# Projecting q and k in two passes of 1024 tokens, each by seven products of half matrices

## The chip, the cores and the metric

The kernel runs on one core of a Trainium2 chip. A core has a matrix engine (TensorE, PE in the profile; its weight loads are listed as PEld), a vector engine (VectorE, DVE), a scalar engine (ScalarE, ACT), GpSimd (POOL) and SyncE (SP), which issues most of the transfers; transfers can also be issued from the queues of ScalarE and of GpSimd. Each engine runs its instructions in the order in which they were written and waits on semaphores for the others. The metric is the device time of one execution in microseconds, lower is better.

## The reference: attention and a routed expert layer, mixed by a gate

The input x has 2048 tokens of 1024 numbers, in fp32. Three things are computed from it:

```
g = sigmoid((x * gate_w).sum(-1))                 # one number per token
q, k, v = split(x @ wqkv)                         # 32 heads of 32 columns each
a = softmax(q k^T / sqrt(32)) v, heads joined, @ wo
b = for each token and each of 32 heads: the best of 8 first keys and the best of 8
    second keys give an expert of 64;  sum of gelu(x . u[e]) * v[e]
out = g * a + (1 - g) * b
```

The part that is changed is `x @ wqkv` for q and k (1024 columns each), the sums of the gate, and a bound on the scores that the softmax uses as its shift.

## The kernel before

**Precision.** A number is kept as two parts, hi (a copy in the matrix engine's fast 32-bit format, made by ScalarE) and lo (number minus hi, by VectorE); the helper `split` (lines 92 to 94) issues both. A product of two matrices is three matmuls: hi by hi, hi by lo and lo by hi.

**The stages.** In order: q and k are projected and stored to DRAM in hi and lo parts (lines 99 to 360); the router's matmuls over 16 tiles of 128 tokens (`router_mm`, L394), beside which VectorE and GpSimd find each token's experts; the values v (from line 625, seven products of half matrices there already: class `Halves`, L617); attention, head by head (L968, L978, L989); the output projection.

**The projection.** x lies transposed (features on the partitions) in SBUF, all 2048 tokens, as hi and lo parts (`xh`, `xl`, four tiles of 512 tokens each). q and k have eight chunks of 128 columns each. Chunk 0 of both is computed while x arrives: for each of the eight 128-feature rows of x (`kc`), ScalarE and VectorE split the row (`split_x`), and TensorE runs 24 matmuls on it (`mm0`, L213), into eight PSUM banks. The other 14 chunks (loop at L322) are four blocks each of 24 matmuls (L329): 56 blocks. The weights of a chunk are loaded two chunks ahead (`load_w`) and split (`split_w`). After each block, `evac` (L135) splits the result into hi and lo, takes the largest absolute value of hi (L141) and keeps the running maximum per column (`amax`); the stores to DRAM go out on ScalarE's queue one block later.

**What lies between the blocks.** The router's keys are folded into its weights: 32 steps of `fold` (L267), four at a time after every fourth block (blocks 8, 12, ... 36), each with a 1 MB load (`load_wq`, four buffers) and four fp32 matmuls with 32 weight columns (L274). After four of them the sum is copied (`wt`, L280), transposed on TensorE one block later (`fold_t`, L288), copied again (L291) and stored. From block 40 on, VectorE adds up x times the gate's weights (`gate`, L311 and L313: 64 instructions of 512 columns); four matmuls in the router stage sum that over the partitions (`gate_sums`, L464). From block 42 the router's weights are loaded back and split (L356).

**The bound.** For each head, the sum over its 32 columns of max|q| times max|k| is an upper bound of its scores (lines 363 to 370 and `bound`, L448). If any bound is above a limit, `exact_maxima` (L475) computes the real maxima in a long extra stage; with these inputs it is jumped over.

The order of the work is written out by hand: what each engine does next is the order of the calls in the code.

## Time and profile before

| | |
|---|---|
| median of 3 runs (lowest to highest) | 1852.4 us (1852.29 to 1852.59) |
| the profiled execution | 1853.26 us, of which the profile's span is 1851.4 us |
| TensorE's first projection matmul | 6.68 us after the span's start |
| the router's first matmul (the projection is over) | 390.60 us |
| TensorE busy in the span | 99% |
| granted TensorE clock, mean | 1.000 |

The profile's page gives, for each engine, its busy time; the span in 40 slices with the busy share of each engine in tenths; and groups of instructions by line of the code, with the count, the busy time, the mean duration of one, and how long the engine stood idle just before them, with the instruction that ended most of that wait. A matmul's duration includes the pipeline; matmuls overlap, so that the distance from one start to the next is what one costs. The timeline lists single instructions by start and duration in microseconds; idle time and what ended it stand in brackets.

### The profile page before, as it was taken

The numbers are of one execution on the slowest core, as the hardware profiler recorded it, in microseconds if no ns is written. First come the engines' busy times: TensorE is split into PE (matmuls) and PEld (weight loads), VectorE is DVE, ScalarE is ACT, GpSimd is POOL, SyncE is SP. The second block draws the span as 40 slices with busy tenths as digits, with TensorE's granted clock in tenths as the row PEclk, the third lists the DMA queues.
The fourth block names the chain that finished last, engine by engine and source line by source line (L and its number), as shares of the span: only waits on it lengthen the run. The fifth ranks groups of instructions, "written<-read, shape, count | busy, mean of one in ns | idle before, by whom it ended". The sixth has DMA issues, their size and how long they took to land.

```text
span 1851.4 us, 26129 instructions
## 1 busy us (share of the span) xinstructions
PE 1841.2 (99%) x10131; PEld 1128.1 (61%) x10131; DVE 1365.8 (74%) x1219; ACT 1198.3 (65%) x1492; POOL 170.1 (9%) x214
## 2 busy tenths in 40 slices
PE   9999999999999999999999999999999999999999
PEld 7877777887888744444444444444444444447787
DVE  4522224978887788888888888888888888896674
ACT  4211111201233399999999999999999999993221
POOL 0000000025401100000000000000000000000000
PEclk9999999999999999999999999999999999999999
DMA  5777784423237687767777777877777777875851
GB/s 216 284 255 257 271 286 136 135 66 105 80 123 249 244 186 159 175 153 174 164 172 178 167 185 162 187 164 178 177 164 175 161 180 167 181 158 181 288 176 57
DMA packets 122853, 332.10 MB, mean 179 GB/s; under 512 B 15988, under 2 KB 57220, under 8 KB 98472
## 3 DMA queue, kind: packets, MB, share of 16 engines
q1 hardware_dynamic: 85048, 180.58, 31.9%
q0 software_dynamic: 17584, 112.08, 28.0%
q10 hardware_dynamic: 20096, 37.76, 6.5%
q8 instruction: 80, 1.31, 0.3%
q14 instruction: 45, 0.37, 0.1%
HBM read 158.65 MB, written 72.10 MB: 125 GB/s over the span
## 4 chain that ended last, share of the span: by engine, by line
PE 60%; DMA 3%; ACT 1%; DVE 0%; issue 0%; SPq 0%; DVEq 0%; ACTq 0%
PE ring L968 27%; PE o L989 25%; PE pa L617 6%; PE ring L1002 1%; DMA accd<-P 1%; DMA out<-rb 1%; DMA accd<-rd 1%; PE pa L1180 1%; DMA rb<-rd 1%; DMA smd<-ssb 0%; ACT P L978 0%; SPq L75 0%; PE pa L1173 0%; DVE V L1242 0%; DMA V<-od 0%
## 5 line engine op out<-in xcount | busy, mean ns | idle before, releaser
L978 ACT ACTIVATE P<-ring 128x1024 f32<-128x1024 f32 (+2 forms) x1031 | 912.4, 983 | 14.7 <-DMA accd<-P 2.6
L1018 DVE TENSOR_TENSOR acc<-acc,P 128x2048 f32<-128x2048 f32 x319 | 731.0, 2291 | 75.1 <-ACT P L978 49.6
L989 PE MATMUL o<-P,V 128*32 128x512 f32 x3840 | 464.8, 599 | 0.0
L968 PE MATMUL ring<-Q,K 98*128 98x512 f32 x1024 | 272.0, 407 | 0.1
L968 PE MATMUL ring<-z,z 98*128 98x512 f32 x1020 | 270.9, 407 | 0.7 <-ACT accd L978 0.6
L968 PEld LDWEIGHTS ring<-Q,K 98*128 98x128 f32 x1024 | 182.0, 188 | 144.2 <-ACT P L978 73.3
L968 PEld LDWEIGHTS ring<-z,z 98*128 98x128 f32 x1020 | 181.2, 188 | 143.4 <-ACT P L978 71.0
L989 PEld LDWEIGHTS o<-P,V 128*32 128x32 f32 x3840 | 98.8, 109 | 223.0 <-issue 214.1
L93 ACT ACTIVATE hi<-bk 128x512 fp32r<-128x512 f32 x64 | 37.6, 598 | 242.1 <-PE bk L329 226.7
L94 DVE TENSOR_TENSOR lo<-bk,hi 128x512 fp32r<-128x512 f32 x64 | 44.2, 690 | 182.2 <-ACT hi L93 178.1
L329 PE MATMUL bk<-xh,whi 128*128 128x512 f32 x448 | 176.2, 393 | 0.1
L329 PE MATMUL bk<-xh,wlo 128*128 128x512 f32 x448 | 174.4, 389 | 0.0
L329 PE MATMUL bk<-xl,whi 128*128 128x512 f32 x448 | 174.4, 389 | 0.0
L1011 POOL DMA_DIRECT2D accd<-P x95 | 81.5, 858 | 930.1 <-ACT P L978 356.3
L1016 DVE TENSOR_TENSOR acc<-P,P 128x2048 f32<-128x2048 f32 x32 | 73.4, 2293 | 72.8 <-ACT P L978 72.8
L329 PEld LDWEIGHTS bk<-xh,whi 128*128 128x128 f32 x448 | 84.1, 188 | 24.1 <-issue 6.7
L329 PEld LDWEIGHTS bk<-xh,wlo 128*128 128x128 f32 x448 | 84.1, 188 | 17.8
L329 PEld LDWEIGHTS bk<-xl,whi 128*128 128x128 f32 x448 | 84.2, 188 | 17.1
L1021 DVE TENSOR_TENSOR acc<-acc,accd 128x2048 f32<-128x2048 f32 x32 | 73.1, 2285 | 0.0
L978 ACT ACTIVATE accd<-ring 128x1024 f32<-128x1024 f32 (+2 forms) x64 | 62.2, 1032 | 2.5 <-PE ring L968 2.4
L617 PE MATMUL pa<-woh,acc 128*128 128x512 f32 x192 | 62.2, 389 | 0.0
L398 ACT ACTIVATE xu<-bk 128x64 f32<-128x64 f32 x16 | 3.6, 224 | 76.5 <-PE bk L394 76.5
(246 smaller groups left out, 1862.5 us busy)
## 6 DMA issues: line engine op xcount, KB each, us to landing
accd<-P POOLq DMA_DIRECT2D x95, 1024.0 KB, 7.6
wqt<-in_wq SPq DMA_DIRECT2D x32, 1024.0 KB
z<-kdh SPq DMA_DIRECT2D x32, 256.0 KB
z<-qdh SPq DMA_DIRECT2D x32, 256.0 KB
V<-vd SPq DMA_DIRECT2D x32, 256.0 KB
K<-kdh SPq DMA_DIRECT2D x32, 256.0 KB
Q<-qdh SPq DMA_DIRECT2D x32, 256.0 KB
od<-osb SPq DMA_DIRECT2D x32, 256.0 KB
```

The costliest lines, as they stand in the source:

```text
L93: nc.scalar.activation(hi, src, AF.Copy)
L94: (on or nc.vector).tensor_tensor(out=lo, in0=src, in1=hi.bitcast(F32), op=OP.subtract)
L329: nc.tensor.matmul(ps, a[:, kc, :], b[n][:, kc, :], start=first, stop=last)
L617: nc.tensor.matmul(ps, self.a[a][i][:, k, :], self.b[b][j][k], start=(not first and k == 0 and i == j == 0), stop=(k == HC - 1 and i == 1))
L968: on_ring(nc.tensor.matmul(ring[:, i, :], K[:98, kt * 128:(kt + 1) * 128], Q[:98, qc * 512:(qc + 1) * 512], start=True, stop=True), i)
L978: on_ring(nc.scalar.activation(P[h, kt][:, q0 * 512:(q0 + m) * 512].rearrange("p (a m) -> p a m", a=m), ring[:, i:i + m, :], AF.Exp, scale ...
L989: nc.tensor.matmul(O[h][32 * qc:32 * qc + 32, :], Vt[g][:, kt, 32 * j:32 * j + 32], p[:, qc * 512:(qc + 1) * 512], start=(kt == 0), stop=( ...
L1002: yield nc.tensor.matmul(ps[32 * qc:32 * qc + 32, :], ones, src[:, qc * 512:(qc + 1) * 512], start=(src is srcs[0]), stop=(src is srcs[-1]))
L1011: nc.gpsimd.dma_start(ACCD[h], P[h, kt], accum_op=OP.add)
L1016: nc.vector.tensor_add(ACC[h], P[h, 0], P[h, kt])
L1018: nc.vector.tensor_add(ACC[h], ACC[h], P[h, kt])
L1021: nc.vector.tensor_add(ACC[h], ACC[h], ACCD[h])
```

## The change

The projection is done in two passes of 1024 tokens: the second half of the tokens first, then the first half. In a pass, q chunk c and k chunk c together are a matrix of 2 x 2 weight quarters A11, A12 (q, features 0 to 511 and 512 to 1023), A21, A22 (k), and x is one of 2 x 2 quarters B11, B12 (features 0 to 511, tokens in two groups of 512), B21, B22. Their product is computed as seven products of quarters (P1 to P7, function `product`, 12 matmuls each) instead of eight, with four sums of weight quarters (S1 to S4, made for every chunk on VectorE, then split) and four differences of quarters of x (T1 to T4, made once a pass on VectorE, then split). The results are joined by seven additions on VectorE per chunk. A pass has eight steps: step 0 and step 8 (`plain_mm`) use the eight plain products, with the quarters of x as they are split; steps 1 to 7 and 9 to 15 are `unit`s with seven products. The second pass takes the chunks in reverse order, so that steps 7 and 8 share weights.

Within a unit the weights of the next unit are summed and split, one quarter after each product, in single places. `evac` splits a result; a Square on ScalarE with a running sum (`accum_out`) takes the place of the maxima on VectorE, one evacuation later together with the stores (`run_late`). The bound becomes the root of the product of the sums of squares over 512 tokens, its maximum over the four groups; the limit is as it was.

The folds go two at a time, after 13 of the steps and in the middle of units 4, 10 and 13, with two loads of 1 MB after each (four half-size buffers, that is, as much as one such fold uses). The copy `wt` is put in the place of `u4`, and the transposes stand right after P1 of the next unit.

The gate's sums become 32 fp32 matmuls per pass with one weight column and 256 tokens each, on the raw x (`gate_sums`), before the last eighth of step 0 and before step 8. The 64 instructions on VectorE and the four matmuls in the router stage go.

At the end of the first pass the second half of x is loaded and split in unit 7 (hooks of unit 7). The parts of x that the router and the values need are made again: one quarter in unit 15 (`split_n1`), four in the router stage at tiles 1, 2, 3 and 5 (`split_rx`), from five loads of 1 MB. The router's weights are split in unit 15.

The core of the diff:

```diff
+    PASS = (dict(B11="xh3", B21="xl0", B22="xl1", B12="xh0", T1="xl2", T2="xh0", T3="xh2", T4="xh1",
+                 ra="xh1", rb="xh2"),
+            dict(B11="xh0", B21="xl0", B22="xl1", B12="xh2", T1="xh1", T2="xh2", T3="xl2", T4="xh3",
+                 ra="xh3", rb="xl2"))
+    TOK0 = (S // 2, 0)
...
+    sq = const.tile([128, 2, KC, NQ], F32, name="sq")
...
-    def evac(which, c, n, ps, parts):
-        m = parts[0].shape[1] // 512
-        hi, lo = (t[:, n % m * 512:(n % m + 1) * 512] for t in parts)
-        split(hi, lo, ps)
-        mx = ev.tile([128, 1], F32, name="m", bufs=8)
-        nc.vector.tensor_reduce(mx, hi.bitcast(F32), axis=AX.X, op=OP.max, apply_absolute_value=True)
-        am = amax[:, which, c:c + 1]
-        if n == 0:
-            nc.vector.tensor_copy(am, mx)
-            nc.vector.tensor_max(am, am, mx)
-        store_parts()
-        if n % m == m - 1:
-            for dst, t in zip(QKD[which], parts):
-                stores.append((dst[128 * c:128 * c + 128, (n + 1 - m) * 512:(n + 1) * 512], t))
...
+    CHUNK = list(range(KC)) + list(range(KC))[::-1]
...
+    def x_parts(place, src=None, pool=None):
+        t = (pool or (xp8 if place == "xl3" else xp)).tile([128, 2, HC, 512], F32R, name=place)
+        if src is not None:
+            split(t[:, 0], t[:, 1], src)
+        return t[:, 0], t[:, 1]
+    def x_quarter(p, name):
+        X[name] = x_parts(PASS[p][name], XR[name], xp)
+    def x_sum(p, name):
+        a, b = dict(T1=("B12", "B11"), T3=("B22", "B12"), T2=("B22", "T1"), T4=("B21", "T2"))[name]
+        out = dict(T1="B11", T3="B12", T2="B22", T4="B21")[name]
+        XR[name] = XR[out]
+        nc.vector.tensor_tensor(out=XR[name], in0=XR[a], in1=XR[b], op=OP.subtract)
...
+    def x_raw_at(kc, c):
+        n, c = divmod(c, 512)
+        return XR[f"B{1 + kc // HC}{1 + n}"][:, kc % HC, c:c + 256]
+    def gate_sums(p):
+        pz = bank_at(6)
+        for kc in range(KC):
+            for q in range(4):
+                nc.tensor.matmul(pz[32 * q:32 * q + 1, :256], gw[:, kc, :], x_raw_at(kc, 256 * q),
+                                 start=(kc == 0), stop=(kc == KC - 1))
+        for q in range(4):
+            row = slice(32 * q, 32 * q + 1)
+            nc.scalar.activation(XR["zs"][row, :], pz[row, :256], AF.Copy)
+            c = TOK0[p] + 256 * q
+            dma(ZD[:, c:c + 256], XR["zs"][row, :], nc.gpsimd)
...
+    def w_sum(u, name):
+        r = wraw[u]
+        a, b, op, out = dict(
+            S1=("A21", "A22", OP.add, None), S2=("S1", "A11", OP.subtract, "A11"),
+            S3=("A11", "A21", OP.subtract, None), S4=("A12", "S2", OP.subtract, "A21"))[name]
+        a, b = r[a], r[b]
+        r[name] = r[out] if out else wr.tile([128, HC, 128], F32, name=name, bufs=1)
+        nc.vector.tensor_tensor(out=r[name], in0=a, in1=b, op=op)
+    def w_parts(u, name, src=None):
+        split(*w_place(name), wraw[u][src or name])
...
+    late = []
+    def run_late():
+        for f, *a in late:
+            f(*a)
+        late.clear()
+    def squares(out, src, which, c, n):
+        nc.scalar.activation(out, src, AF.Square, accum_out=sq[:, which, c, n:n + 1])
+    def evac(which, c, n, src, ps):
+        hi, lo = (ev.tile([128, 512], F32R, name=part) for part in ("hi", "lo"))
+        split(hi, lo, src)
+        run_late()
+        late.append((squares, ps, src, which, c, n))
+        for dst, t in zip(QKD[which], (hi, lo)):
+            late.append((dma, dst[128 * c:128 * c + 128, n * 512:(n + 1) * 512], t, nc.scalar))
...
+    PLAIN = {(0, 0): "A11", (0, 1): "A12", (1, 0): "S4", (1, 1): "A22"}
...
+    FACTORS = dict(P1=("A11", "B11"), P2=("A12", "B21"), P3=("S4", "B22"), P4=("A22", "T4"),
+                   P5=("S1", "T1"), P6=("S2", "T2"), P7=("S3", "T3"))
+    def product(name):
+        ps = bank_at(prod_no[0] % 6)
+        prod_no[0] += 1
+        a, b = (m[f] for m, f in zip((AW, X), FACTORS[name]))
+        for k in range(HC):
+            for i, j in ((0, 0), (0, 1), (1, 0)):
+                nc.tensor.matmul(ps, a[i][:, k, :], b[j][:, k, :],
+                                 start=(k == 0 and i == j == 0), stop=(k == HC - 1 and i == 1))
+        return ps
...
+    def fold():
+        for _ in range(2):
+            if i == 0:
+                fold_ps[:] = [bank_at(6)]
+            t = wq_t.pop((n, 0)), wq_t.pop((n, 1))
+            for quad in range(4):
+                nc.tensor.matmul(ps[32 * quad:32 * quad + 32, :], kpad[:, quad % 2, i, :],
+                                 t[quad // 2][:, quad % 2, :], start=(i == 0), stop=(i == 3))
+        if i == 3:
+            wt = ev.tile([128, 512], F32, name="u4", bufs=1)
+            nc.scalar.activation(wt, ps, AF.Copy)
+            pending.append((n // 4, wt))
+        for m in range(n + 1, min(n + 3, 32)):
...
+        if kc == 3:
+            load_w(1)
+        if kc == 4:
+            for n in range(2):
+                load_wq(n)
+        if kc == 5:
+            w_sum(1, "S1")
+            w_sum(1, "S3")
+            w_parts(1, "S1")
+            kpad_diffs()
         if kc == KC - 1:
-            split_w(0, 1)
-            load_w(1, 1)
-
-            xr.close()
-            ev0 = Pool("ev0")
-        order = [(n, i) for i in range(3) for n in range(NQ)]
+            gate_sums(0)
+            x_sum(0, "T1")
+            x_quarter(0, "T1")
+            w_parts(1, "A11")
+            w_sum(1, "S2")
+            w_parts(1, "S2")
+            w_sum(1, "S4")
+            w_parts(1, "S4")
+            for name in ("T3", "T2", "T4"):
+                x_sum(0, name)
...
+    def plain_evac(u, w, n):
+        evac(w, CHUNK[u], TOK0[u // KC] // 512 + n, b0[w, n], b0[w, n])
+    def after_plain(u, done):
+        rest = [(w, n) for n in range(2) for w in range(2) if (w, n) not in done]
+        p, v = u // KC, u + 1
+        x_quarter(p, "T2")
+        plain_evac(u, *rest.pop(0))
+        w_parts(v, "A12")
+        plain_evac(u, *rest.pop(0))
+        first, second = rest[:1], rest[1:]
+        hooks[v, "P1"] = [(plain_evac, u, *a) for a in first] + [(w_parts, v, "S3")]
+        hooks[v, "P5"] = [(x_quarter, p, "T3"), (w_parts, v, "A22")]
+        hooks[v, "P6"] = [(x_quarter, p, "T4")] + [(plain_evac, u, *a) for a in second] + [(load_w, u + 3)]
...
+    FOLDS = {1, 2, 3, 4, 5, 6, 8, 9, 10, 11, 12, 13}
+    MID_FOLDS = {4, 10, 13}
...
+    def unit(u):
+        p, c, v = u // KC, CHUNK[u], u + 1
+        n0 = TOK0[p] // 512
+        seven = v < NUNIT and v != KC
+        def ready(name, f=w_parts, *args):
+            if seven:
+                w_parts(v, name)
+        def hook(name):
+            for f, *a in hooks.pop((u, name), []):
+                f(*a)
+        if v + 1 < NUNIT and u % KC != 1 and v + 1 != KC:
+            load_w(v + 1)
+        p1 = product("P1")
+        c1 = place("c1")
+        nc.scalar.activation(c1, p1, AF.Copy)
+        run_late()
+        fold_t()
+        hook("P1")
+        if seven:
+            w_sum(v, "S1")
+            w_sum(v, "S3")
+        ready("A11")
+        p5 = product("P5")
+        ready("S1")
+        if seven:
+            w_sum(v, "S2")
+        hook("P5")
+        p6 = product("P6")
+        u2, u4 = place("u2"), place("u4")
+        add(u2, c1, p6)
+        add(u4, u2, p5)
+        ready("S2")
+        if seven:
+            w_sum(v, "S4")
+        hook("P6")
+        p2 = product("P2")
+        add(c1, c1, p2)
+        evac(0, c, n0, c1, p2)
+        if u in MID_FOLDS:
+            fold()
+        ready("A12")
+        hook("P2")
+        p7 = product("P7")
+        u7 = place("u7")
+        add(u7, u4, p7)
+        add(u2, u2, p7)
+        evac(1, c, n0 + 1, u7, p7)
+        ready("S3")
+        hook("P7")
+        p3 = product("P3")
+        add(u4, u4, p3)
+        evac(0, c, n0 + 1, u4, p3)
+        ready("S4")
+        hook("P3")
+        p4 = product("P4")
+        add(u2, u2, p4)
+        evac(1, c, n0, u2, p4)
+        ready("A22")
+        hook("P4")
+        if u in FOLDS:
+            fold()
...
+    hooks[5, "P1"] = [(next_raw, "r21")]
+    hooks[6, "P1"] = [(load_a21,)]
+    hooks[7, "P1"] = [(next_raw, "ra")]
+    hooks[7, "P5"] = [(next_raw, "rb")]
+    hooks[7, "P2"] = [(x_quarter, 1, "B11")]
+    hooks[7, "P7"] = [(x_quarter, 1, "B12")]
+    hooks[7, "P3"] = [(w_parts, 8, "S4", "A21"), (x_quarter, 1, "B21")]
+    hooks[7, "P4"] = [(x_quarter, 1, "B22")]
+    for u in range(1, KC):
+        unit(u)
+    plain_banks(1)
+    load_w(KC + 2)
+    gate_sums(1)
+    for ki, n in ((0, 0), (0, 1), (1, 0), (1, 1)):
+        for w in range(2):
+            for k in range(HC):
+                for i in range(3):
+                    plain_mm(w, n, ki * HC + k, i, ki == k == i == 0, ki == 1 and k == HC - 1 and i == 2)
+        nxt = KC + 1
+        if (ki, n) == (0, 0):
+            x_sum(1, "T1")
+            x_quarter(1, "T1")
+        elif (ki, n) == (0, 1):
+            for name in ("S1", "S3"):
+                w_sum(nxt, name)
+            w_parts(nxt, "A11")
+            w_parts(nxt, "S1")
+            w_sum(nxt, "S2")
+            w_parts(nxt, "S2")
+            for name in ("T3", "T2", "T4"):
+                x_sum(1, name)
+        elif (ki, n) == (1, 0):
+            for w in range(2):
+                plain_evac(KC, w, 0)
+            w_sum(nxt, "S4")
+            w_parts(nxt, "S4")
+    after_plain(KC, ((0, 0), (1, 0)))
+    fold()
...
+    hooks[14, "P1"] = [(load_n1,)]
+    hooks[14, "P4"] = [(open_rw,)]
+    for kc, name in enumerate(("P1", "P5", "P6", "P2", "P7", "P3", "P4")):
+        hooks[15, name] = [(split_wp, kc)]
+    hooks[15, "P6"].append((split_n1,))
+    hooks[15, "P4"].append((split_wp, 7))
+    for u in range(KC + 1, NUNIT):
+        unit(u)
...
+    nc.vector.tensor_reduce(amax, sq, axis=AX.X, op=OP.max)
     nc.vector.tensor_mul(pr, amax[:, 0, :], amax[:, 1, :])
+    nc.scalar.activation(pr, pr, AF.Sqrt)
...
-    def gate_sums():
-        pz = bank()
-        for qc in range(NQ):
-            nc.tensor.matmul(pz[32 * qc:32 * qc + 32, :], ones, zacc[:, qc * 512:(qc + 1) * 512],
...
+        if t in (1, 2, 3, 5):
+            ni, ki = {1: (2, 0), 2: (2, 1), 3: (3, 0), 5: (3, 1)}[t]
+            split_rx(ni, ki)
+            if ni == 2:
+                load_rx(3, ki)
```

358 lines of the change are left out of this document (182 added, 176 removed).

## The prediction

> **What bounds the kernel now.** I read the page first (engines, slices), then TensorE's waits, the stage's stretches and the timeline.
>
> ```profile
> span 1851.4 us, 26129 instructions
> PE 1841.2 (99%) x10131; PEld 1128.1 (61%) x10131; DVE 1365.8 (74%) x1219; ACT 1198.3 (65%) x1492; POOL 170.1 (9%) x214
> PE   9999999999999999999999999999999999999999
> DVE  4522224978887788888888888888888888896674
> ACT  4211111201233399999999999999999999993221
> ```
> ```profile
> PE bk L213 <- ACT xh L93: 1.2, 1, 1.2
> ...
> PE bk L213 <- DVE xl L94: 0.2, 1, 0.2
> ```
> ```profile
> 20.00:22.50 2.50, 2.50 (x12) 2.06 (x11) 0.80 (x3) 1.36 (x3) 0.00 (x0) 1.00 1.04 437
> ```
> ```profile
> 50.00:75.00 25.00, 24.93 (x110) 20.33 (x109) 17.60 (x40) 7.12 (x14) 0.00 (x0) 1.00 0.88 333
> ...
> 100.00:125.00 25.00, 25.00 (x129) 18.42 (x128) 6.94 (x13) 4.60 (x7) 0.93 (x1) 1.00 0.80 280
> ...
> 400.00:420.00 20.00, 20.00 (x92) 16.28 (x91) 14.50 (x31) 0.98 (x5) 10.44 (x14) 1.00 0.00 0
> ```
>
> TensorE is busy throughout; in the projection it waits 1.4 us in all, for the first x. VectorE and ScalarE have a quarter and a fifth of that stage's time to do (6.94 and 4.60 of 25 us). So a matmul less is time won as long as the other two keep up; the change gives them the work.
>
> **The change part by part: TensorE.**
>
> ```profile
> 6.68 0.50 PE L213 MATMUL bk<-xh,whi 128*128 128x512 f32 x1 [1.20 <-ACT xh L93]
> ...
> 22.29 1.07 PE L213 MATMUL bk<-xl,whi 128*128 128x512 f32 x4
> ...
> 44.05 1.07 PE L213 MATMUL bk<-xl,whi 128*128 128x512 f32 x4
> ```
> ```profile
> 100.72 3.64 PE L274 MATMUL bk<-wqt,kpad 128*32 128x512 f32 x32
> ...
> 109.86 0.60 PE L288 MATMUL bk<-ident,wt 128*128 128x128 f32 x4
> ```
>
> Between 22.29 and 44.05 us lie 96 matmuls: 0.2267 us each. Before there are 64 blocks of 24, 1536. After: 2 x 96 plain and 14 units of 84, 1368. The 168 less are 38.1 us. The Trainium skill (TensorE: Matmul & The Clock Gate, "Wait — 56ns, not 53.3ns?") gives N/2.4 GHz plus 2.5 ns, 216 ns for 512 columns, an estimate of 36.3 us; the row decides. The router's four gate matmuls save 0.9 (16 of this kind, two records each, in 3.64 us). The new gate's sums are 64 of 256 columns: 7.3 us if the time goes by columns, 14.6 if by instruction; I take 9, 4.5 a pass, near the first because four run side by side in the row too. Work: -38.1 - 0.9 + 9 = -30.0 us.
>
> **VectorE and ScalarE, steady units.**
>
> ```profile
> L94 DVE TENSOR_TENSOR lo<-bk,hi 128x512 fp32r<-128x512 f32 x64 | 44.2, 690 | 182.2 <-ACT hi L93 178.1 <-DMA qdl<-lo 4.0
> L93 ACT ACTIVATE hi<-bk 128x512 fp32r<-128x512 f32 x64 | 37.6, 598 | 242.1 <-PE bk L329 226.7 <-DVE lo L94 11.2 <-DMA qdh<-hi 4.2
> L313 DVE SCALAR_TENSOR_TENSOR zacc<-xl,ugr,zacc 128x512 f32<-128x512 f32 x32 | 21.9, 745 | 0.0
> L94 DVE TENSOR_TENSOR xl<-xl,xl 128x2048 fp32r<-128x2048 f32 x3 | 6.9, 2285 | 0.0
> L93 ACT ACTIVATE xl<-xl 128x2048 fp32r<-128x2048 f32 x3 | 5.7, 1916 | 0.0
> L623 DVE TENSOR_TENSOR xl<-xl,xh 128x2048 f32<-128x2048 f32 x1 | 2.3, 2286 | 0.0
> ```
> ```profile
> 22.41 12.13 DVE L94 TENSOR_TENSOR xl<-xraw,xh 128x512 fp32r<-128x512 f32 x20
> ```
> ```profile
> 110.06 0.60 ACT L93 ACTIVATE hi<-bk 128x512 fp32r<-128x512 f32 x1 [5.04 <-PE bk L329]
> 110.07 0.34 ACTq L75 DMA_DIRECT2D qdh<-hi  x1
> 110.50 0.39 ACTq L75 DMA_DIRECT2D qdl<-lo  x1
> 110.94 0.55 ACT L291 ACTIVATE wt<-bk 128x448 f32<-128x448 f32 x1 [0.28 <-ACT hi L93]
> ```
>
> A unit gives VectorE 22 instructions of 512 columns: 4 sums, 7 lo parts of weights, 7 additions, 4 lo parts of results. In a row they cost 0.61 us (20 in 12.13), 13.4 in all. Three times an addition, hi and lo form a chain in which VectorE waits 0.65 us for ScalarE, and three times ScalarE has a Square and two stores (0.85, the stores' issue as in the last rows) ahead of the next hi: about 18.4 us a unit (19.4 with the fold's copies). TensorE needs 84 x 0.2267 = 19.0, 21 with a fold (1.82). So steady units stay TensorE's, with 1.6 us a unit to catch up a lag; if the chain were 1 us longer than TensorE's unit, each of the 12 full units would cost 1 us. The gate's 64 instructions and the maxima that leave VectorE stood beside a busy TensorE: they are worth nothing.
>
> What is tightest are the transposes behind P1, in every second unit. They need `wt`, which ScalarE copies behind P4's evacuation and A22's hi. P7's and P3's evacuations take 3.4 us each against 2.72 of a product, so the two engines are 1.3 us behind at P4; then addition, hi, Square with stores, A22's hi and the copy, 3.3. `wt` is ready 4.6 us after P4, TensorE is there after fold and P1, 4.5. With waits of about 0.3 us in six units I count 2 (0 to 5).
>
> Transfers: a unit moves 1 MB of weights, 2 MB for the folds and 2 MB of stores, 250 GB/s over 21 us, where 437 was reached: hidden, but for the places below.
>
> **The start: 4.5 us.**
>
> ```profile
> 7.85 3.16 ACTq L75 DMA_DIRECT2D w0raw<-in_wqkv  x3
> 11.06 0.51 ACT L93 ACTIVATE whi<-w0raw 128x128 fp32r<-128x128 f32 x2 [2.87 <-DMA xraw<-in_xT]
> ...
> 16.03 0.42 ACT L93 ACTIVATE whi<-w0raw 128x256 fp32r<-128x256 f32 x1 [1.51 <-DMA w0raw<-in_wqkv]
> ...
> 21.14 0.63 ACT L93 ACTIVATE whi<-w0raw 128x512 fp32r<-128x512 f32 x1 [2.08 <-DMA w0raw<-in_wqkv]
> ```
>
> A row of x now holds 12 matmuls, 2.72 us, not 5.44, but the first weights come through ScalarE's queue: their last piece was split at 21.14, ahead of row 3 of x in ScalarE's order, which TensorE now wants at 15.3. With half of x ahead of it the piece comes earlier; 1.5 to 8 us, I take 4.5. TensorE ends row 6 near 31 us: 6.7, seven rows of 2.72, 0.5 of the first row's own waits, 4.5.
>
> **First pass: T1 to T4.** T1 overwrites raw x that the gate's sums read, so VectorE starts it halfway through them. Up to T2's lo: T1 2.29, its hi 1.92, lo 2.29, five weight instructions 3.0 with two waits 1.3, T3, T2 and T4 6.9, T2's lo 2.29: 20 us. TensorE meanwhile: half of the gate 2.25, row 7 2.72, fold 1.82, P1 and P5 5.44: 12.2, and P6 needs T2. Stall 7.5 (6 to 9). From there to T3's lo: ten instructions 6.1 (three results of step 0, A12, S3, two sums, A11, S1, the sum S2), T3 2.29, ScalarE's lag 1.5, against P6 and P2, 5.44: stall 4.5 (3 to 6). With that much VectorE is still behind when unit 1 ends, and next late is `wt` in unit 2: seventeen instructions 10.4, T4 2.29, waits for ScalarE in the evacuations of P2, P3 and P4 4.7, A22's hi and the copy 1.2: 18.6 us after T3, against P7, P3, P4, fold and P1, 12.7: 5.8 (3 to 7.5). Queued behind each of these waits is all of TensorE's work; whatever lag is left after unit 2 no later place asks for.
>
> **Second pass.** In unit 7 SP's queue issues 2 MB for the folds, 1 MB of weights, then, after P1, 2 MB of x; with the stores some 6.55 MB until x is there, at 437 to 333 GB/s 15.0 to 19.7 us after the unit's start; I take 17.9. ScalarE stands at B11's hi until then, and behind it the evacuations of P7 and P3. From there VectorE and ScalarE make B11, P7's evacuation, B12, P3's, A21, B21, P4's, B22 (23.8 us, each quarter 1.92 + 2.29 behind one another), then T1 6.5, five weight instructions 3.0 and 1.3, T3, T2, T4 6.9, two evacuations 1.2, S4 1.9, T2 with its hi 3.4: 24.2. T2 is ready at 65.9. TensorE: unit 7 19.6 with transposes, gate 4.5, 96 matmuls 21.8, fold 1.8, P1, P5 5.4: 53.1. Stall 12.8 (9 to 16), then T3 2.9, then `wt` in unit 10 5.1 (2.5 to 7).
>
> **Folds in mid unit, router.** The load after a middle fold has 8.2 us (P7, P3, P4) for 2.1 MB beside 0.8 of stores, 6.6 to 8.7 us by those two rates: 1 us each, 3 (0 to 10). The four splits in the router stage, 9.2 us of VectorE, lie in its idle time (5.5 of 20 us above): 0; uncovered they would delay the values by up to 5. The bound worked out from the inputs is 113 at most, the limit 30 x sqrt 32 = 169.7: the long extra stage stays jumped over.
>
> **Sum:** -30.0 + 4.5 + 7.5 + 4.5 + 5.8 + 12.8 + 2.9 + 5.1 + 2 + 3 = +18.1 us. The profiled execution took 1853.26 us (1.9 more than its span), the median 0.86 less; the difference put on the median gives 1870. All low bounds together, with 7.3 for the gate, come to -5; all high ones to +50.
>
> **The rivals.** (1) Faster: the pass starts are covered. If VectorE reached T2's parts before the weight sums and T3, T4 (or ran ahead of ScalarE), P6 would wait for 13 us of work (T1 6.5, T2's difference 2.3, hi and lo 4.2), not 20, and the chains behind would shrink likewise: about 6 of the 38.6 us of these six stalls stay, and the sum is -15: 1837. It decides at T2: ready before P5 ends. Against it: ScalarE's weight copy at 48.56 us stood 16.36 us for a place with other work behind it, so the written order holds.
>
> ```profile
> 48.56 1.06 ACT L93 ACTIVATE whi<-wraw 128x1024 fp32r<-128x1024 f32 x1 [16.36 <-PE bk L213]
> ```
>
> (2) No change: the same chains, some 18 us shorter in sum (near all the low bounds together), 1852. (3) Slower still by the clock:
>
> ```profile
> L288 PE MATMUL bk<-ident,wt 128*128 128x128 f32 x32 | 4.8, 272 | 0.0
> ...
> L209 PE MATMUL bk<-ident 128*128 128x128 f32 x22 | 4.1, 365 | 1.4 <-DVE ident L89 1.4
> ```
>
> The same form took 365 ns at the start, after idling, and 272 later; if each of six gaps brings 4.1 us at that pace, 1 us each, up to 6: 1876, less where VectorE is late anyway. Against: the granted clock is 1.00 in every row above, but none has such a gap. The Trainium skill (same page, "Part 1: The HAM clock gate" and "Why this matters for your kernels") says one idle window of about 3.4 us halves the clock: 1.7 us a gap, an estimate of up to 10. (4) The gate's sums go by instruction, 14.6 us, in part behind waits, and the folds' loads reach their upper bound: 1885.
>
> **How the numbers follow.** Forecast 0.50 (1858 to 1882), (1) 0.24, (2) 0.07, (3) 0.10, (4) 0.09. Within 0.2% (1848.7 to 1856.1, about what can be told from no change) is (2); slower 0.69. Half of (1) and the tail of (4) are left out: 1842 to 1888.
>
> **What would show it.**
>
> ```profile
> 390.37 0.39 PE L329 MATMUL bk<-xh,wlo 128*128 128x512 f32 x1
> 390.60 0.39 PE L394 MATMUL bk<-wph,xh 128*128 128x512 f32 x1
> ```
>
> Right: the router's first matmul near 408 us instead of 390.6; TensorE idle ahead of P6 and P7 in units 1 and 9, released by VectorE's lo of T2 and T3, ahead of the transposes in units 2 and 10, and in step 8 by A21. Wrong: a router start below 390, no idle above 3 us at P6, or idle spread over all units (then the steady unit is VectorE's).

## The result: 1.6% slower, and where the time went

The changed kernel takes 1881.8 us (median of 4, 1880.62 to 1883.51) against 1852.5 us before (1852.29 to 1853.07): the ratio is 1.0158, its 95% interval 1.0141 to 1.0176. The profiled execution took 1882.36 us, its span 1880.6. The page of the changed kernel begins like this (engines with busy time, share and instructions; then tenths of busy time in 40 slices of 47 us):

```profile
span 1880.6 us, 26511 instructions
...
PE 1835.0 (98%) x10083; PEld 1106.0 (59%) x10083; DVE 1470.5 (78%) x1276; ACT 1315.2 (70%) x1730; POOL 182.7 (10%) x224
...
PE   8799889999999999999999999999999999999999
...
DVE  5766486668987878888888888888888888896674
...
PEclk9899989999999999999999999999999999999999
```

TensorE is busy 6 us less than before, although 168 matmuls are gone, and its idle time stands in the slices at the start of each pass, where the granted clock is lower too. Behind the router everything is as it was. The router's first matmul is the first mark, the first matmul of the values (line 887) the second:

```profile
413.67 0.50 PE L641 MATMUL bk<-wph,xh 128*128 128x512 f32 x1 [0.46 <-ACT bk L222]
...
508.48 3.79 PE L887 MATMUL bk<-xh,xh 128*128 128x512 f32 x16
```

The first was at 390.60 before, the second at 479.92. So the projection is 23.1 us longer, the router stage 5.5 (94.8 against 89.3), and the rest 0.6. The view of TensorE's waits (total, times, longest) names the places:

```profile
PE bk L267 <- ACT xh L94: 8.9, 2, 5.5
PE bk L267 <- ACT bk L222: 6.2, 1, 6.2
PE bk L255 <- ACT S L94: 5.4, 1, 5.4
PE bk L267 <- DVE xh L95: 3.3, 2, 1.7
PE bk L317 <- ACT u L305: 2.5, 1, 2.5
PE bk L641 <- ACT wph L94: 2.1, 2, 1.7
```

**First pass.** TensorE's timeline in unit 1, products P6, P2, P7, P3:

```profile
51.02 0.80 PE L267 MATMUL bk<-xh,S 128*128 128x512 f32 x1 [5.50 <-ACT xh L94]
53.54 4.49 PE L267 MATMUL bk<-xh,S 128*128 128x512 f32 x11 [1.73 <-DVE xh L95]
57.87 2.88 PE L267 MATMUL bk<-xl,A 128*128 128x512 f32 x12
...
66.98 4.82 PE L267 MATMUL bk<-xh,S 128*128 128x512 f32 x12 [6.23 <-ACT bk L222]
71.68 3.03 PE L267 MATMUL bk<-xl,S 128*128 128x512 f32 x12
```

P6 waits for T2's hi (5.50) and lo (1.73). P7 waits 6.23, but not for T3: its bank is freed by a Square (L222). On ScalarE that Square stands behind T4's hi and the fourth result's hi:

```profile
63.93 1.91 ACT L94 ACTIVATE xh<-x 128x2048 fp32r<-128x2048 f32 x1 [1.39 <-DVE xh L95]
...
65.75 0.58 ACT L94 ACTIVATE hi<-bk 128x512 fp32r<-128x512 f32 x1
66.22 0.59 ACT L222 ACTIVATE bk<-bk 128x512 f32<-128x512 f32 x1
```

The distances say something else as well. From 53.54 to 57.87 the 11 matmuls take 0.39 us each, from 66.98 to 71.68 the 12 take the same: half the pace of 0.2267. In the stretches (TensorE, weight loads, VectorE, ScalarE, GpSimd busy, granted clock, transfers) the clock shows it:

```profile
25.00:50.00 25.00, 18.79 (x133) 11.15 (x131) 17.18 (x21) 8.30 (x14) 1.95 (x4) 1.00 0.46 163
50.00:75.00 25.00, 16.03 (x50) 12.04 (x51) 21.64 (x26) 15.81 (x28) 0.00 (x0) 0.73 0.49 136
75.00:100.00 25.00, 25.00 (x127) 18.50 (x129) 16.63 (x26) 12.42 (x27) 0.81 (x1) 1.00 0.77 251
...
250.00:275.00 25.00, 18.18 (x61) 13.43 (x60) 20.65 (x24) 14.84 (x23) 0.00 (x0) 0.80 0.62 181
```

VectorE has 21.64 of 25 us to do where TensorE stands still, and 16.63 where it does not: the pass starts are VectorE's (with its waits for ScalarE), the steady units TensorE's.

**Second pass.** ScalarE's timeline (raw x), and TensorE's (k half of step 8, P6 of unit 9, transposes of unit 10):

```profile
211.25 1.91 ACT L94 ACTIVATE xh<-xh 128x2048 fp32r<-128x2048 f32 x1 [9.22 <-DMA xh<-in_xT]
```
```profile
223.94 4.84 PE L255 MATMUL bk<-xh,S 128*128 128x512 f32 x12 [5.44 <-ACT S L94]
228.62 2.88 PE L255 MATMUL bk<-xh,A 128*128 128x512 f32 x12
...
256.06 0.80 PE L267 MATMUL bk<-xh,S 128*128 128x512 f32 x1 [3.40 <-ACT xh L94]
258.39 4.48 PE L267 MATMUL bk<-xh,S 128*128 128x512 f32 x11 [1.53 <-DVE xh L95]
...
285.20 0.66 PE L317 MATMUL bk<-ident,u 128*128 128x128 f32 x4 [2.50 <-ACT u L305]
285.61 7.34 PE L267 MATMUL bk<-xh,S 128*128 128x512 f32 x24
```

SP's queue (SyncE's issues) shows when raw x was asked for:

```profile
193.00 5.74 SPq L76 DMA_DIRECT2D wraw<-in_wqkv  x2
198.84 2.07 SPq L76 DMA_DIRECT2D xh<-in_xT  x4
```

Raw x lands at 211.2, some 22 us after unit 7's start (188.94). Behind it hang A21's parts, T2 and, in unit 10, the fold's copy; after the waits the matmuls are slow again, 0.39 us each in two of these products and 0.30 on the mean of the 24 in unit 10.

**Router stage.** The first tile waits for the parts of its last two weight rows, and at 470.31, behind the ninth tile, for VectorE at the branch on the score bound (before, there: 0.30, for ScalarE):

```profile
420.55 0.50 PE L641 MATMUL bk<-wph,xl 128*128 128x512 f32 x1 [1.75 <-ACT wph L94]
...
470.31 0.47 PE L641 MATMUL bk<-wph,xh 128*128 128x512 f32 x1 [1.24 <-DVEq L722]
```

The first tile takes 10.3 us (413.67 to 424.00) instead of 24 x 0.2267 = 5.4, the second, which begins at half pace, 6.4 (to 430.36). These 5.8 us are about the 5.5 by which the stage is longer; the branch (0.9 more) and the gate's four matmuls that are gone (0.9 less) cancel. The splits of x in this stage come later (the first on ScalarE at 430.68).

### The profile page after: what moved, and what is told of

The parts are those of the page before. It is cut to its first block, busy times and chain, and to the rows that moved or that the text cites. A ratio compares the mean times of both kernels' runs of the same rounds, so it can differ in the third digit from the quotient of the medians.

```text
span 1880.6 us, 26511 instructions
## 1 busy us (share of the span) xinstructions
PE 1835.0 (98%) x10083; PEld 1106.0 (59%) x10083; DVE 1470.5 (78%) x1276; ACT 1315.2 (70%) x1730; POOL 182.7 (10%) x224
## 4 chain that ended last, share of the span: by engine, by line
PE 66%; DVE 3%; DMA 3%; POOL 1%; issue 1%; ACT 1%; SPq 0%; DVEq 0%; ACTq 0%; POOLq 0%
PE ring L1220 27%; PE o L1241 25%; PE pa L868 6%; PE bk L868 6%; PE ring L1254 1%; POOL eq L655 1%; DMA accd<-P 1%; DMA out<-rb 1%; DMA accd<-rd 1%; PE pa L1432 1%; DVE eq L664 0%; DMA smd<-ssb 0%; DVE mm L662 0%; DVE vt L95 0%; DVE m L649 0%
## 5 line engine op out<-in xcount | busy, mean ns | idle before, releaser
L1263 POOL DMA_DIRECT2D accd<-P x95 | 81.5, 858 | 930.4 <-ACT P L1230 364.0
L267 PE MATMUL bk<-xh,S 128*128 128x512 f32 x336 | 88.8, 419 | 18.4 <-ACT xh L94 8.9
L267 PEld LDWEIGHTS bk<-xh,S 128*128 128x128 f32 x336 | 67.7, 204 | 36.0 <-ACT xh L94 9.7
L267 PE MATMUL bk<-xl,S 128*128 128x512 f32 x336 | 82.6, 398 | 1.9 <-DVE xl L95 1.8
L267 PE MATMUL bk<-xh,A 128*128 128x512 f32 x336 | 83.0, 396 | 1.1 <-DVE A L95 1.1
L267 PEld LDWEIGHTS bk<-xh,A 128*128 128x128 f32 x336 | 62.0, 188 | 25.2 <-issue 10.1
L94 ACT ACTIVATE hi<-u 128x512 fp32r<-128x512 f32 x42 | 26.5, 632 | 69.4 <-DVE u L448 66.3
L267 PEld LDWEIGHTS bk<-xl,S 128*128 128x128 f32 x336 | 63.6, 191 | 18.0 <-DVE xl L95 2.1
L95 DVE TENSOR_TENSOR A<-wraw,A 128x512 fp32r<-128x512 f32 (+2 forms) x47 | 31.3, 667 | 34.3 <-ACT A L94 33.3
L94 ACT ACTIVATE xh<-xh 128x512 fp32r<-128x512 f32 (+1 forms) x25 | 24.2, 986 | 39.5 <-DVE xh L850 20.0
```

The lines of the kernel that those rows point to most:

```text
L94: nc.scalar.activation(hi, src, AF.Copy)
L95: (on or nc.vector).tensor_tensor(out=lo, in0=src, in1=hi.bitcast(F32), op=OP.subtract)
L267: nc.tensor.matmul(ps, a[i][:, k, :], b[j][:, k, :], start=(k == 0 and i == j == 0), stop=(k == HC - 1 and i == 1))
L1263: nc.gpsimd.dma_start(ACCD[h], P[h, kt], accum_op=OP.add)
```

## The experiments

Single executions of the changed kernel lie 2.9 us apart, so that for runs of one execution the marks in the trace are compared; those timed in rounds have an interval. Marks vary too: in the run with the router's weights earlier, which changes nothing ahead of unit 14, TensorE was 3.4 us later at the end of unit 15 (P4 at 413.71, 410.33 in the changed kernel). So a difference of a few microseconds in one execution counts here only where the rows next to the edit show it. Line numbers in a trace are those of its own kernel.

### Raw x of the second pass early

```diff
-FOLDS = {1, 2, 3, 4, 5, 6, 8, ...};  MID_FOLDS = {4, 10, 13}
+FOLDS = {1, 2, 3, 4, 5, 8, ...};     MID_FOLDS = {4, 5, 10, 13}
-hooks[7, "P7"] = [(x_quarter, 1, "B12")]
+hooks[7, "P7"] = [(load_w, KC + 1), (x_quarter, 1, "B12")]   # no longer at unit 7's start
```

> Raw x of the second pass is issued ahead of the weights of unit 9, and the fold at the end of unit 6 is moved to the middle of unit 5, so that its 2 MB are out of the way. Theory (the second pass starts late because raw x lands 22 us after unit 7's start, and VectorE's and ScalarE's chain hangs on it): x lands near 198 us instead of 211, B11's hi starts behind the evacuation of P2 near 202, the whole chain up to T2's lo is 9 us earlier (from 256.0 to 247), the gate's sums and step 8's k half do not wait (7.5 us of waits and 2 us at half clock go), and TensorE waits at P6 of unit 9 for what is left; the router's first matmul 8 to 9 us earlier, total about 1873. Rival (VectorE and ScalarE have too much to do in any case, the landing is covered): the router's first matmul within 2 us of 413.7, total 1880 to 1882.

```profile
204.84 1.92 ACT L94 ACTIVATE xh<-xh 128x2048 fp32r<-128x2048 f32 x1 [2.24 <-DMA xh<-in_xT]
```
```profile
217.53 4.86 PE L255 MATMUL bk<-xh,S 128*128 128x512 f32 x12 [1.65 <-ACT S L94]
```

x lands 6.4 us earlier, at 204.84, not at 198. T2's lo is 6.4 us earlier (249.64), the router's first matmul 6.5 (407.18), the total 1876.1: what the landing gains arrives whole, so the theory holds and the rival falls; the gain was put too high because x still took 12 us from its issue at 193.08. The run moves the weights and a fold's 2 MB together, so it does not say which of the two held x up. Ahead of P6 of unit 9 TensorE waits as long as before (3.36 us): the chain behind x has its own length. And the matmuls behind a wait of only 1.65 us still run at half pace.

### The bank of P7

```diff
-hooks[v, "P6"] = [(x_quarter, p, "T4")] + [(plain_evac, u, *a) for a in second] + [(load_w, u + 3)]
+hooks[v, "P6"] = [(plain_evac, u, *a) for a in second] + [(x_quarter, p, "T4"), (load_w, u + 3)]
```

> The fourth result of step 0 is evacuated ahead of T4's split, so the Square that frees P7's bank in unit 1 runs some 3 us earlier. Theory (VectorE's work up to the copy in unit 2 binds, the bank is only where the wait shows): P7 of unit 1 starts near 64 us instead of 67, the transposes in unit 2, which did not wait, now wait 2 to 3 us; total the same within 1 us. Rival (the bank is the cause): nothing is given back, total about 3 us less.

```profile
63.84 4.62 PE L267 MATMUL bk<-xh,S 128*128 128x512 f32 x12 [2.98 <-ACT bk L222]
71.84 5.49 PE L267 MATMUL bk<-xl,S 128*128 128x512 f32 x12 [3.38 <-ACT bk L222]
77.12 3.16 PE L267 MATMUL bk<-xh,A 128*128 128x512 f32 x12
```

P7 is 3.1 us earlier, and P3 then waits 3.38 for the next bank, whose Square comes one evacuation later, behind T4's parts; P4 is 2.6 us later than in the changed kernel (74.55). Total 1884.5. P3 begins where it did before (71.84 against 71.68): the bank was where the wait showed, not its cause. I had expected the time back at the transposes; it came back one product on.

### The gate's sums row by row

```diff
-            gate_sums(0)                 # 32 matmuls ahead of row 7
+        if 2 <= kc < KC - 1:             # rows 2 to 6 (and the last part in row 7)
+            for k in ((0, 1, 2) if kc == 2 else (kc,)):
+                gate_mm(k)
```

> The gate's sums of the first pass are issued row by row (rows 2 to 7), in the places where TensorE waits for the split of x, instead of in one piece ahead of row 7. Theory (T1's difference waits for the gate's sums, and VectorE's chain behind it binds the first pass): the sum T1 starts near 29 us instead of 32.0, everything up to the transposes of unit 2 is 3 us earlier, total about 3 us less. Rival (TensorE's own 3.6 us for the sums is what counts, and rows 2 to 7 have no room): first plain matmul of row 7 no earlier than 33, total the same.

```profile
27.85 2.28 DVE L142 TENSOR_TENSOR xh<-xh 128x2048 f32<-128x2048 f32 x1
35.86 2.29 DVE L95 TENSOR_TENSOR xl<-xh,xl 128x2048 fp32r<-128x2048 f32 x1 [5.72 <-ACT xl L94]
```

The difference T1 starts 4.2 us earlier, its lo only 1.45 (37.31 before): T1's hi stands on ScalarE behind the copies of the gate's sums, which wait for the last of them. Unit 2 starts 0.7 us earlier; the total, 1883.0, shows nothing of it (one execution). A step of the chain was moved and the next engine's order kept the rest.

### Filling TensorE's waits

```diff
+    def filler(ps, n):                   # results that nobody reads
+        for _ in range(n):
+            nc.tensor.matmul(ps, hi[:, 0, :128], hi[:, 0, :], start=True, stop=True)
```

20 ahead of P6 and 24 ahead of P7 in unit 1, 20 ahead of step 8's k half, 11 ahead of P6 in unit 9.

> Four of TensorE's waits are filled with matmuls whose results nobody reads: 20 ahead of P6 and 24 ahead of P7 of unit 1, 20 ahead of the k half of step 8, 11 ahead of P6 of unit 9 (0.2267 us each, none longer than the wait it stands in). Theory of the clock (idle windows halve the matrix clock, and that adds to the time): the 12 matmuls behind each of the four places take 2.7 us instead of 4.5 to 4.8, total 4 to 8 us less. Rival (VectorE binds in these stretches, so that TensorE's pace does not matter): the same shorter products, but the time comes back as longer waits further on, at the transposes of units 2 and 10 above all; total within 1 us of 1881.8. If the slow products are no matter of the clock, they stay at 4.5 us.

```profile
61.28 5.60 PE L266 MATMUL bk<-xh 128*128 128x512 f32 x24
66.72 2.88 PE L278 MATMUL bk<-xh,S 128*128 128x512 f32 x12
71.22 3.02 PE L278 MATMUL bk<-xl,S 128*128 128x512 f32 x12 [1.62 <-ACT bk L222]
```

Behind two of the four fillers (P7 of unit 1, step 8) the product runs at full pace, 2.0 us less each; the two P6, which still waited about 2 us for T2's lo behind the filler, stay slow. So idle time does halve the pace. But little of the 3.9 us won arrives. P3 now waits 1.62 for a bank, since VectorE and ScalarE are no earlier, and unit 2 starts 40.8 us after unit 1 as before (37.98 to 78.75, 38.42 to 79.22). From step 8's k half to unit 10 it is 55.1 us instead of 55.7. The router's first matmul is 1.2 us earlier (412.43), 0.4 of which unit 1 had at its start, ahead of the fillers. Total 1883.6. The clock is real, and in these places mostly not what the time costs.

### Eight plain products in units 1 and 9

```diff
-    for u in range(1, KC):
+    plain_unit(1)           # results (0,1), (1,1), (0,0), (1,0), 24 matmuls each
+    for u in range(2, KC):
         unit(u)
```

T2 is split behind the second result, T3 behind the third, T4 ahead of the fourth's evacuation; S1 to S4 of unit 2 in between. Likewise for unit 9.

> Units 1 and 9, the first behind each pass's start, are computed as eight plain products (96 matmuls instead of 84, results (0,1), (1,1), (0,0), (1,0) in that order), so that T1 to T4 and the sums S1 to S4 are wanted one unit, 22 us, later; nothing else changes. Theory (VectorE and ScalarE cannot make T1 to T4 and the weights in the time of one step, and TensorE waits for them, partly at half clock): TensorE's waits in units 1, 2, 9 and 10 go, with them the slow products (18 us in the first pass, 13 in the second), for 2 x 2.72 us of work; the wait for A21 in step 8 stays. Router's first matmul near 388, total about 1856. Rival (VectorE and ScalarE are short of time in the whole projection, so that the wait only moves): waits of the same sum appear in units 2 to 4 and 10 to 12, total 1880 or more.

```profile
73.75 1.12 PE L317 MATMUL bk<-ident,u 128*128 128x128 f32 x4 [8.09 <-ACT u L305]
```

All waits for T1 to T4 go, for 24 matmuls more. The router starts at 398.81, 14.9 us earlier, the total is 1869.9. That is the direction of the theory and somewhat over half its size (14.9 of 25.7 us): part of the wait returns in one place, ahead of the transposes of unit 2 (8.09) and 10 (3.90), for which ScalarE's copy comes behind T3's and T4's parts.

### The router's weights earlier, and all three together

```diff
-    for kc, name in enumerate(("P1", "P5", "P6", "P2", "P7", "P3", "P4")): ...   # one split each, the 8th behind P4
+    for kc, name in enumerate(("P1", "P1", "P5", "P5", "P6", "P6", "P2", "P7")): ...
```

> The splits of the router's weights are issued one to two products earlier in unit 15 (two each behind P1, P5 and P6, one behind P2 and P7) and the split of the last quarter of x at the end of unit 14. Theory (the first router tile waits for its last two weight rows, and runs at half clock behind that): the first tile takes 5.4 us instead of 10.3, the values start 94.8 - 5 = 90 us behind the router's first matmul, total 1876 to 1877. Rival (the loads of these rows from DRAM are late, not the splits): the first tile still waits, total above 1880.

```profile
421.36 0.80 PE L640 MATMUL bk<-wph,xh 128*128 128x512 f32 x1 [4.76 <-ACT bk L222]
```
```profile
410.49 0.58 ACT L94 ACTIVATE wph<-wpr 128x448 fp32r<-128x448 f32 x1 [3.21 <-DMA wpr<-wpd]
```

The rival's cause holds, at another place: ScalarE now stands 3.21 and 2.19 us for the loads of rows of which two at a time fit into their buffers, the evacuations of unit 15 come late behind it, and the router's first bank is not free (4.76). The first tile itself no longer waits for a weight row; it takes 7.9 us, slow behind the wait for the bank. Total 1884.2, nothing gained.

> Raw x of the second pass early, units 1 and 9 in eight products, and the router's weights early, all three. If the three causes are separate their gains add: -6 for raw x (the waits of step 8), -25 for the two plain units, -5 for the router: about 1845 to 1848, below the kernel before. If the plain units already cover the late x, the first gain falls away: 1851.

The three together: 1865.2 us, 1.0065 of before (1.0048 to 1.0081), 14 us above the higher of the two forecasts. The gain of the early x is there (router's first matmul 3.7 us earlier than with the plain units alone, 4.9 of wait for its bank included); 11.9 us of waits for the transposes and 4.9 for the bank remain.

### Another order around the plain units

```diff
+        for j, (w, n, ki) in enumerate(((0, 1, 0), (1, 1, 0), (0, 1, 1), (1, 1, 1), (0, 0, 0), ...
+            if j == 1:      # B12 is done
+                x_sum(p, "T4"); x_quarter(p, "T2"); ...; x_quarter(p, "T3"); plain_evac(u - 1, 0, 1)
...
+        fold()              # its copy ahead of the last result
+        evac(1, c, n0, ps[1, 0], ps[1, 0])
...
+    bank_no[0] = 6          # the router's first bank
```

> The version with all three, and the work around the plain units put in another order: the blocks that read B12 come first, so that T2's place is free 5 us earlier; T2, T3 and T4 are split before the results and weights that are wanted later; the fold's copy comes ahead of the last result; the router's first bank is one that is long free. Theory (what was left were waits in single places: 8.1 and 3.9 us for the transposes of units 2 and 10, 4.9 us for the router's bank, 1.2 for A11, slow products behind them): these go, about 18 us less than the 1865 measured, 1846 to 1850, below the kernel before. Rival (VectorE and ScalarE are full there, and the order only moves the wait): the waits reappear at S2, T3 or a bank in units 2 and 10, total 1860 or more.

```profile
443.27 0.76 PE L662 MATMUL bk<-wph,xh 128*128 128x512 f32 x1 [7.02 <-DVEq L743]
```

1857.1 us, 1.002 (1.001 to 1.003). The router starts at 385.27, 5.3 us earlier than in the kernel before: the projection is faster at last. What it wins is paid in the router stage, which takes 97.9 us (before 89.3): VectorE enters it late, has the splits of x to do there, and at the branch TensorE waits 7.02 and goes on at half pace. The time fits neither forecast: the wait went to a place that neither had named.

### Three single waits less

```diff
+        for kc in range(6): load_wp(kc)          # 4 of them into places of later lo parts
+        evac(0, c, n0 + 1, ..., ("c1", "u2"))    # one result of the plain units in free places
```

and the gate's sums row by row.

> The version with the new order, and three single waits of it taken away: six of the eight router weight rows are loaded at once (into places of later rows' lo parts) instead of two at a time, so that VectorE does not enter the router stage 10 us late; the gate's sums of the first pass go row by row; one result of the plain units is kept in two places that are free there, so that a store is not waited for. Theory (VectorE's lag into the router stage is what TensorE pays with 7.0 us and a slow stretch at the branch on the score bound; the store buffers delay ScalarE by 3.5 us, which TensorE pays in unit 4): the wait at the branch falls below 2 us, the one in unit 4 below 1; 1844 to 1849. Rival (the router stage's own work on VectorE, 4.6 us a tile and nine long splits, makes the lag): the wait at the branch stays above 5 us, 1851 to 1855.

```profile
110.61 0.34 ACTq L76 DMA_DIRECT2D qdl<-lo  x1
110.99 0.63 ACT L94 ACTIVATE A<-wraw 128x512 fp32r<-128x512 f32 x1 [2.88 <-DMA wqt<-in_wq]
111.53 0.58 ACT L313 ACTIVATE u<-bk 128x512 f32<-128x512 f32 x1
```
```profile
112.16 1.11 PE L325 MATMUL bk<-ident,u 128*128 128x128 f32 x4 [3.37 <-ACT u L313]
112.93 5.47 PE L275 MATMUL bk<-xl,S 128*128 128x512 f32 x12
```

1852.2 us, 0.9996 (0.9987 to 1.0005): not to be told from the kernel before, and the best of these versions. The branch still costs 4.4 us, between the theory's 2 and the rival's 5, unit 4 3.37 and a product at half pace. ScalarE's timeline shows why: the issue of a store (qdl) went through only at 110.61, 3.4 us behind the one before it, while the fold's four loads were being taken, and the copy that the transposes need stands two places behind it. The row with 2.88 names a load of the fold's weights as what came last, though this split reads none of them. The semaphores in the trace settle it: the store's issue waits for semaphore 104, the one that it will raise itself, and the fold's load issued at 104.97 under the same number raised it for the last time at 110.58. ScalarE's stores and SP's loads take turns on eight semaphores in this program (100, 102 to 104, 115 to 118).

### The stores on GpSimd's queue

```diff
-            late.append((dma, dst[...], t, nc.scalar))
+            late.append((dma, dst[...], t, nc.gpsimd))
```

> As the version before it, with the stores of q and k issued from GpSimd's queue instead of ScalarE's. Theory (in units 2 to 4 ScalarE stood 0.4, 2.4 and 2.9 us at the issue of a store, each time beside the fold's four loads, and what it does next came late by that; TensorE paid in unit 4 with 3.4 us and a slow product of 4.2): ScalarE's gaps at the issue go, TensorE's wait in unit 4 falls below 0.5 us, total 4 to 6 us less, 1846 to 1848, below the kernel before. Rival (the gap is the store buffers, which come free no sooner on any queue): the gap moves to ScalarE's hi copies, total within 1.5 us of 1852.

```profile
PE bk L309 <- DMA wqt<-in_wq: 9.0, 6, 2.6
```

1860.6 us, 1.004 (1.0025 to 1.0054): worse; the router starts 8.0 us later than in the lean version (393.59 against 385.64). The wait in unit 4 is gone, and ScalarE's splits of A no longer stand behind one (2.7 us for transposes in all, 6.3 before the edit), but TensorE now waits 9.0 us for the folds' loads (1.0 before). GpSimd's transfers have eight semaphores of their own (106 to 113), so that ScalarE and its stores are rid of the loads. Both runs move the same on the mean (245 and 244 GB/s from 40 to 385 us). That the transfers share one supply, and the queue only chooses who is late, is how I read it; no run shows it.

> The changed kernel with that one edit alone: stores from GpSimd's queue. If ScalarE's issues matter at the starts of the passes too, where its hi copies and VectorE's lo parts follow one another, the router's first matmul comes 2 to 4 us earlier than 413.7; if VectorE's own work binds there, within 1 us.

On the changed kernel alone: router's first matmul at 414.81, total 1880.1. No gain; that fits VectorE's work binding there, but one execution does not prove it.

### The fold's loads one at a time

```diff
-        for m in range(n + 1, n + 3): load_wq(m)
+        load_wq(n + 1);  hooks[u + 1, "P6"].append((load_wq, n + 2))
-FOLDS, MID_FOLDS = {1, ..., 5, 8, ...}, {4, 5, 10, 13}
+FOLDS, MID_FOLDS = {1, ..., 6, 8, ...}, {6, 12, 13}
```

> The lean version (stores from ScalarE's queue again), with the fold's loads one at a time: 1 MB behind a fold, the second 1 MB behind a product of the next unit, those behind unit 6 only after raw x; the folds in the middle of units 4, 5 and 10 moved to 6 and 12, away from the starts; and each router weight row split in one instruction instead of two. Theory (ScalarE's store issues stand still while 2 MB of fold loads are in the queues, and TensorE pays in unit 4): the wait for the transposes of unit 4 (3.4 us) and the slow product behind it (1.4) go, the fold's own waits stay below 1 us in sum, 1845 to 1848. Rival (the transfers as a whole are what is short in these units: 2 MB of fold loads, 1 MB of weights and 2 MB of stores in each): the waits move to the folds, 1851 to 1854.

```profile
PE bk L685 <- DVEq L766: 4.9, 1, 4.9
PE bk L310 <- DMA wqt<-in_wq: 3.8, 3, 2.1
PE bk L329 <- ACT u L314: 2.7, 2, 1.4
```

1854.4 us, 1.0005 (0.9996 to 1.0015). The rival again: the wait in unit 4 goes, 2.8 us more are waited for the folds' loads, 2.3 in step 8 for A21's parts (none in the lean version), and the branch is at 4.9 (4.4). None of the versions beats the kernel before.

## Why the prediction was right, and which sizes were off

Slower was right, by the mechanism named: chains of VectorE and ScalarE at the two pass starts, behind raw x. The size was 12 us short: 1870 against 1881.8. That this lies inside the range (1858 to 1882), by 0.2 us, is luck: the second pass and the router stage erred by 6 to 7 us each, and the start of the first pass came right for partly other reasons than those given. Point by point, measured from one start to another, less 0.2267 us for each matmul:

| step | forecast, us | measured, us |
|---|---|---|
| 168 matmuls less | -38.1 | -38.1; a unit with fold and transposes takes 21.65 (79.22 to 100.87) |
| gate's sums | +9 | +7.1; 30.06 to 33.63 is 3.57 for 32: by columns, the lower bound |
| the start | +4.5 | +4.4 behind the first matmul, which itself came 0.6 earlier (6.07 against 6.68); row 6 ended at 30.06, not 31 |
| T2, T3, `wt` in units 1 and 2 | +17.8 | +19.9, of which 3.8 at half pace (38.42 to 77.36 for 84 matmuls) |
| second pass to unit 10 | +20.8 | +27.6 (gate 3.2, step 8 7.8, unit 9 11.9, unit 10 4.7), of which 7.3 at half pace |
| steady `wt`, middle folds | +5 | about +3, what is left over; not as waits but 0.1 to 0.2 us at every fold and transpose |
| projection | +19.0 | +23.1 |
| router stage | -0.9 | +5.5 |

- **First pass.** T2 at P6, 7.5 forecast, was 7.2. **T3 at P7 was the wrong name**: its lo was ready at 63.84, the Square at 66.8. The prediction counted Squares as ScalarE's time and overlooked that each holds a PSUM bank until the next evacuation. The bank run shows that the sum did not hang on it: with the bank free 3 us earlier P3 still began at 71.84, behind T4's parts. `wt` in unit 2, 5.8 forecast, came out at none because the wait had been had earlier. The sum of the three was good, their places were not; and of the 19.9 the waits at P6 and P7 are 13.5, the rest half pace (3.8), a wait for A11's lo (1.1) and what lies between, so that part of the agreement is luck.
- **Second pass: the term that was mis-sized.** Raw x was taken to land 17.9 us after unit 7's start and landed at 22, outside its bounds (15.0 to 19.7): they were made of bytes over bandwidth, while SP issued x only 9.9 us into the unit (198.84), behind two issues of weights that took 5.74. The second of these, at 198.41, stood for semaphore 116, which a load for the folds issued at 189.09 raised for the last time at 198.40. The early-x run shows that each microsecond of it arrives whole. These 4 us are more than half of the 6.8 by which the term was short; half pace (7.3 us in this stretch) stood in no term of the sum, so other parts of the stall were put too high.
- **The clock** was held as a rival (0.10) of 6 us. Counted over the six slow stretches of the projection (11 matmuls in 4.33 us in P6 of unit 1, and so on) it is 11.1 us, 1.7 to 2.0 in each. The filler run shows that a good part of it runs while VectorE is late anyway, so how much of it belonged in the sum stays open. The size that the prediction worked out from the Trainium skill (TensorE: Matmul & The Clock Gate, "Part 1: The HAM clock gate"), 1.7 us a gap, an estimate, was nearer than the 1 us from the rows.
- **The router stage was the step that failed outright**, by a term that the sum lacked: the router's weights, split in unit 15. The parts of the last two rows come behind P4's evacuation on ScalarE and VectorE, the last row's load is itself late (ScalarE waits 1.06 for it, at 421.56), and the first tile pays 4.9 us, the second 0.9 at half pace. The 0 for the splits of x in "idle time" nearly held: VectorE is busy 81.5 of 94.8 us there against 71.5 of 89.3 before, which is mostly these splits, and what it is late by shows at the branch alone, 1.24 us against 0.30. In the versions with the new order, whose projection is shorter, VectorE enters the stage with more lag, and TensorE waits 2.8 to 7.0 at the branch. The cover was counted over the stage, not up to the places where TensorE waits for the others.
- **Steady units** stayed TensorE's, as forecast: no wait from 84 to 208 us. The prediction's cost for the folds' loads (3 us, up to 10) was not in this trace; 1.98 us at one middle fold came in the run with the router's weights earlier, and up to 9.0 in the leaner versions, where TensorE no longer gave them time.
- **The rival "faster"** asked for T2 before P5's end. With the demand moved a unit later, that is what the last versions do, and the projection is 5 us faster than before. Its forecast of 15 us less for the whole held the gate's sums and the start; it lacked the 24 matmuls that this took (5.4 us) and the router stage.

What stays open: how much of what the router stage costs (4.2 us more than before in the lean version, 8.6 in the one with the new order) could be had by moving the branch or the splits of x, since no run changed them; what of the half pace is on the path in the second pass; and what other semaphores for the stores, on ScalarE's own queue, would give.

## What to carry to other kernels

Before trading matmuls for work on other engines, work out for the first unit after every start when each engine has its inputs, not the shares over the stage: from 40 us to the router VectorE was busy 246 of 374 us and its chains still cost some 47 (19.9 and 27.6) at the two starts. Where such a chain is late, moving one wait moves the time to the next place in the order; what helped was to put the demand off by a whole unit, at the price of a few matmuls, and to bring the first load forward.

## What was not expected of the hardware

- **Half pace after short waits.** Besides waits of 5 and 6 us, one of 2.50 (unit 10), one of 1.82 (P7 of unit 9) and one of 1.65 (early x) were followed by matmuls at half pace; waits of 1.35 and 1.60 us in the lean version were not (12 matmuls in 2.82 us behind the first). The traces' records of the granted clock show why. In each of the 13 traces of changed kernels the clock changes only at multiples of 3.41 us from its first change. Of these steps at full clock (6846 in all), each in which no matmul ran for more than 1.9 us was followed by a step at half clock, none with less than 1.0, and between them both occur. The waits of 2.50, 1.82 and 1.65 lay each within one step; the one of 1.60 was divided between two (0.3 and 1.3). The Trainium skill's rule (same page and section) speaks of an idle window of about 3.4 us that runs freely; the step agrees, but about half a step without matmuls was enough here.
- **An engine's own work can stand at the issue of a transfer.** In the lean version ScalarE, with nothing to wait for but a store's issue, stood 2.4 and 2.9 us while loads of 0.5 MB each from SP's queue were under way. The Trainium skill (DMA: Bandwidth & Descriptors, "Issuing engines are not separate DMA queues") says that transfers of all issuing engines run on the same 16 engines. What held ScalarE at 110.61 was not the queue as such but a semaphore: the store's issue waited for the end of a load with the same number. The 2.4 us end at the issues of 90.97 and 91.94, 0.1 us behind the ends (90.89 and 91.86) of the transfers that had their semaphores before, a store of ScalarE's own (issued at 84.00) and a fold's load (84.23). That the wait in unit 4 went when the stores left ScalarE (the run with GpSimd's queue, which has other semaphores) agrees.
- **A sum along the way costs a second row.** Each Square with `accum_out` is followed by a read of the accumulator of 0.19 us on ScalarE, beside its own 0.59.
